# An order table, v through SyncE's queue, ungated weights and a re-cut w_out in a fused attention and MLP kernel

## Chip, cores and metric

The kernel runs on one core of a Trainium2 chip. The metric is device time of one execution in microseconds (us), the median of three runs.

## What is computed

For batch b and head h a state of 48 x 48 runs over 768 steps: the output at a step is r times (state + (u k) v), then the state becomes w times state + k v. The result, reordered to 3072 tokens of 384 values, goes through two matrix products.

```python
y[:, :, t] = einsum('bhd,bhde->bhe', rt, state + einsum('bhd,bhe->bhde', u[None] * kt, vt))
state = w[None, :, :, None] * state + einsum('bhd,bhe->bhde', kt, vt)
...
h = x @ w_in                 # 384 -> 2048
g = maximum(h, 0) ** 2
out = g @ w_out              # 2048 -> 384
```

The inputs and the output are f32. r, k and v have the shape (4, 8, 768, 48).

## The kernel before, in words

The 768 steps are cut into 6 chunks of 128, and chunk times batch gives 24 **units** (unit i is chunk i // 4, batch i % 4). All state and product work of a unit is done by matmuls over its 128 steps. For each unit the steps are, with the names that the texts below use (the order table's words are the same):

- `rt`, `kt`, `vt`: loads of r, k and v, 192 KB each (lines 430 and 462). r and k go through SyncE's (SP's) hardware queue. Units 0 to 5 load r and k in two halves of 96 KB with long runs, units from 6 on with runs of 192 bytes. v goes through GpSimd's (POOL's) software queue in all units. Before each v load from unit 2 on, POOL copies one element of the k of the unit before (line 465, `gate`), so that v does not start before that load has landed.
- `scale` (DVE, line 453): r and k times powers of w, to bf16.
- Transposes of the scaled r and k. In units 0 to 5 TensorE (PE) does it: `turn` (line 481), eviction `rkT` by ScalarE (ACT), a turn back `kb` with its eviction `kbT`. In units from 6 on a DMA transpose on SP's queue does it (line 473, `rkD` in the table of the change).
- `at` (line 515): eight matmuls over 64 rows. `mask` (DVE, two per unit), `rk` (DVE).
- `sums` (line 535, `s` in the table): four narrow matmuls for the diagonal, four for the new state. `dv`, `sadd`, `sdec` on DVE, `stb` on ACT follow. `vb` (ACT, line 469) casts v to bf16; it is needed by `sums` and `y`.
- `y` (line 569): the output, evicted by `yb` (DVE). It is turned by PE with `xturn` and `xT` in units 0 to 5, by a DMA transpose on SP (`xD`, line 599) in the others.
- `m1` (line 613): four groups of 12 matmuls per unit, weights from `w_in`. Group s uses quarter s of w_in, called I.s. `relu` (ACT) and the squares `sq` (`sqA` on ACT, `sqD` on DVE) follow each group.
- `m2` (line 642): four groups of four matmuls per unit of 384 columns. Group q uses quarter q of w_out, called O.q. `osb` (ACT) evicts, `out` stores through SP's queue. The last unit is done in two halves (line 658).

The eight weight quarters are cast to bf16 by DMAs of POOL's queue (line 441). A `gate` copy ahead of each one waits for some load of r or k (FRONT, line 277).

Every instruction is issued in an order that is worked out when the program is traced: class `Plan` (line 17) holds the steps with costs, ranks and needs, walks a planned clock and emits the steps. `TURNS` (line 197) has ranks that were changed by hand. Engines run their own instruction queues in order: an instruction that waits holds up all that stand behind it on that engine. While PE has nothing to do at the start, the planner puts in `fill` matmuls (line 379, one 128x128 each), 98 in all. `place` says which of eight PSUM banks a step writes.

In the order before, POOL's queue has: vt.0, the mask, vt.1, zeros, the columns of u (`uwb`), vt.2, I.0, vt.3, I.1, `wend`, I.3, I.2, vt.4, O.0 to O.3 and vt.5 on; the weights that each call loads follow the planner's ranks.

Of the kernel before, what the change touches and what calls it, by code (L numbers as in the profile page):

```python
# [16 lines left out]
class Plan:  # L17

    def __init__(self, lags, cold, spare, turns):
        self.turns = turns
        self.lags = lags
        self.cold = cold  # L30
        self.spare = spare
        self.steps = []
        self.at = {}
        self.users = {}
        self.place = {}

    def add(self, key, engine, cost, emit, needs=(), rank=0.0, new=(), uses=(), move=None):
        kind, which = (key[0], key[1] if len(key) == 2 else key[1:]) if isinstance(key, tuple) else ("", key)
        rank = self.turns.get(kind, {}).get(which, rank)
        s = dict(key=key, engine=engine, cost=cost, emit=emit, rank=rank, new=new, move=move)  # L40
        s["needs"] = [n for n in needs if n is not None]
        self.at[key] = s
        self.steps.append(s)
        for x in tuple(new) + tuple(uses):
            self.users.setdefault(x, []).append(s)

    def run(self, room, banks, count):
        todo = {}
        for s in self.steps:
            todo.setdefault(s["engine"], []).append(s)  # L50
        for mine in todo.values():
            mine.sort(key=lambda s: s["rank"])
        rings = {name: [] for name in room}
        free = {e: 0.0 for e in todo}
        queues = {e: [] for e in todo}
        held = {n: None for n in range(count)}
        since = {n: 0.0 for n in range(count)}
        begin, until, tight, loose = self.spare
        free["SP"] = 0.74
        held[0] = "fill"  # L60
        order = []
        t = 0.0
        left = len(self.steps)
        tiny = 1e-9

        moved, chained, left_pe, to_pe, near = self.lags

        def ready(s, e):
            if s["move"]:
                return s["end"] + moved + s["move"][4]  # L70
            if s["engine"] == "PE":
                return s["end"] + (chained if e == "PE" else left_pe)
            return s["end"] + (to_pe if e == "PE" else near)

        marks = []

        def mark(s):
            for e in ("PE", ""):
                heappush(marks, ready(s, e))

        def done(s, e):
            return "end" in s and ready(s, e) <= t + tiny

        def fits(s):
            e = s["engine"]
            names = [x[0] for x in s["new"]]
            for name in set(names):
                if name in banks:
                    continue
                ring, m = rings[name], room[name]  # L90
                for n in range(len(ring) - m, len(ring) - m + names.count(name)):
                    if n >= 0 and not all(done(x, e) for x in self.users[ring[n]]):
                        return False
            wanted = [name for name in names if name in banks]
            if wanted:
                for n, x in held.items():
                    if x not in (None, "fill") and all(done(u, e) for u in self.users[x]):
                        held[n], since[n] = None, max(u["end"] for u in self.users[x])
                if sum(x is None for x in held.values()) < len(wanted):
                    return False  # L100
                for name in set(wanted):
                    mine = sum(x is not None and x[0] == name for x in held.values())
                    if mine + wanted.count(name) > banks[name]:
                        return False
            return True

        while left:
            if held[0] == "fill" and t > until:
                held[0] = None
            for e, mine in todo.items():  # L110
                if free[e] > t + tiny:
                    continue
                if e == "PE" and t < begin - tiny:
                    free[e] = begin
                    continue
                for s in mine:
                    if s["move"] and sum(x[1] / x[0]["move"][0] * x[0]["move"][3] for x in queues[e]) > 1.5:
                        continue
                    if all(done(self.at[k], e) for k in s["needs"]) and fits(s):
                        mine.remove(s)  # L120
                        left -= 1
                        for x in s["new"]:
                            if x[0] in banks:
                                n = 4 + x[1] if x[0] == "log" else min((n for n in held if held[n] is None), key=lambda n: since[n])
                                held[n] = x
                                self.place[x] = n
                            else:
                                rings[x[0]].append(x)
                        s["start"] = t
                        free[e] = t + s["cost"] * (self.cold[1] if e == "PE" and t < self.cold[0] else 1.0)  # L130
                        if s["move"]:
                            queues[e].append([s, s["move"][0], free[e] + s["move"][2]])
                        else:
                            s["end"] = free[e]
                            mark(s)
                        order.append(s)
                        break
                else:
                    if e == "PE" and t < until:
                        free[e] = t + (tight * self.cold[1] if t < self.cold[0] else loose)  # L140
                        order.append(dict(key="fill", emit=self.fill, start=t, end=free[e], engine="PE"))
            heads = [q[0] for q in queues.values() if q]
            moving = [x for x in heads if x[2] <= t + tiny]
            whole = sum(x[0]["move"][1] for x in moving)
            later = [f for f in free.values() if f > t + tiny]
            while marks and marks[0] <= t + tiny:
                heappop(marks)
            later += marks[:1]
            later += [x[2] for x in heads if x[2] > t + tiny]
            later += [t + x[1] * whole / x[0]["move"][1] for x in moving]  # L150
            if not later:
                if left:
                    raise ValueError("nothing can go on: " + str([s["key"] for m in todo.values() for s in m[:3]]))
                break
            step = min(later) - t
            t += step
            for x in moving:
                x[1] -= step * x[0]["move"][1] / whole
                if x[1] <= 1e-7:
                    queues[x[0]["engine"]].pop(0)  # L160
                    x[0]["end"] = t
                    mark(x[0])
        return order
# [3 lines left out]
def kernel(  # L167
# [26 lines left out]
    LATE = (0.2, 0.2, 0.4)  # L194
    MOST = 3
    SQUARES = 'AAAMAAAM'
    TURNS = {
        "": {
            "zeros": 38.551
        },  # L200
        "O": {
            0: 76.019, 1: 91.228, 2: 107.535, 3: 7
        },
        "rt": {
            0: -83.003, 1: -66.162, 12: 22.377, 13: 28.231, 14: 28.49, 15: 33.657, 3: -36.29, 5: 1.476, 8: 3.237
        },
        "kt": {
            0: -80.584, 1: -55.486, 10: 19.508, 11: 20.529, 2: -47.443, 6: 2.358
        },
        "at": {  # L210
            0: -3.958, 11: 34.671, 4: -16.745, 7: 10.944
        },
        "mask": {
            (1, 0): -39.238, (10, 0): 33.02, (2, 1): 25.375, (5, 1): 1.515
        },
        "sadd": {
            1: 9.124, 4: 45.244
        },
        "rk": {
            2: 13.012, 7: 14.32, 8: 68.867, 9: -12.042  # L220
        },
        "sums": {
            11: 49.353, 2: -24.778, 8: 5.082
        },
        "dv": {
            2: -26.848, 7: 34.164, 9: -12.993
        },
        "stb": {
            2: -9.741, 4: 57.421
        },  # L230
        "scale": {
            (10, 0): 23.594, (11, 0): -15.371, (3, 0): -29.763, (4, 0): 33.082, (7, 1): 6.517, (8, 1): 4.379
        },
# [656 lines left out]
```

## Time and profile before

| what | value |
|---|---|
| median of 3 runs (lowest, highest) | 176.56 us (176.39, 176.58) |
| profiled execution, first to last instruction (span) | 174.3 us |
| what lies around the span, by the median | 2.26 us |
| PE busy | 166.7 us, 96% |
| ACT busy, DVE busy, POOL busy | 132.1, 121.1, 40.0 us |
| DMA packets, data | 76474, 28.93 MB |
| share of 16 DMA engines: SP's queue, POOL's queue | 69.8%, 23.9% |

The profiled execution has no time of its own on the page beside its span, so the distance to the median is the difference of the two. PE is TensorE's matmuls, PEld its weight loads, which lie beside the matmuls. The names with a q behind (POOLq, SPq) are the engines' queues that issue DMAs. The chain of waits is followed back from the last instruction to what released it. "To landing" is the time from the issue of a DMA to its completion. The DMA share adds up the times of packets, so it can be above 1 where two queues are served in turn.

### The profile page before, as it was taken

To read this page: it belongs to the slowest core of one execution; us is meant where nothing else is said; L and a number is where in the kernel's file an instruction comes from. 1 tells how busy PE (TensorE), PEld (TensorE's weight loads), DVE (VectorE), ACT (ScalarE), POOL (GpSimd) and SP (SyncE) were. 2 spreads that over 40 slices of the span, in tenths; PEclk is the share of its full clock that TensorE was granted. 3 is DMA by queue.
4 is the path that set the end of the run, shared out by engine and by line. 5 is a ranking of instruction groups with operands and counts; after the bars stand their busy time and mean duration, and the time that the engine had idled before them with its cause. 6 is when DMAs were issued, how large, how long until landed. Compare 5 with 4: busy or idle time off the path is not lost.

```text
span 174.3 us, 5795 instructions
## 1 busy us (share of the span) xinstructions
PE 166.7 (96%) x2390; PEld 134.7 (77%) x2390; DVE 121.1 (70%) x252; ACT 132.1 (76%) x268; POOL 40.0 (23%) x84
## 2 busy tenths in 40 slices
PE   7978899999999999999999999999999999999991
PEld 6766799887687787886896787869787698877871
DVE  7869976615999899977986799794989635531010
ACT  3946999999458797886968876939994869948640
POOL 7866890300140220302032202203202000000000
PEclk9999999999999999999999999999999999999999
DMA  4889999999999999999999999999999971130121
GB/s 97 228 179 246 232 218 193 185 221 118 170 201 164 178 154 209 200 214 170 231 142 183 156 237 214 218 177 141 186 200 175 271 180 26 26 111 6 47 81 56
DMA packets 76474, 28.93 MB, mean 166 GB/s; under 512 B 65440, under 2 KB 75296, under 8 KB 76448
## 3 DMA queue, kind: packets, MB, share of 16 engines
q1 hardware_dynamic: 70848, 20.56, 69.8%
q0 software_dynamic: 5312, 7.87, 23.9%
q8 instruction: 18, 0.29, 0.8%
q10 hardware_dynamic: 288, 0.15, 0.4%
q14 instruction: 8, 0.07, 0.1%
HBM read 20.50 MB, written 4.72 MB: 145 GB/s over the span
## 4 chain that ended last, share of the span: by engine, by line
PE 81%; DMA 11%; SPq 4%; issue 1%; DVE 0%; POOL 0%; POOLq 0%
PE bank L623 35%; PE bank L647 33%; DMA w_in_q<-in_moe_w_in_dram 5%; SPq L436 4%; DMA rkT<-rkw 4%; PE bank L521 4%; DMA rt<-in_r_dram 2%; PE bank L576 2%; PE bank L582 2%; PE bank L546 2%; PE bank L663 2%; PE bank L541 1%; PE bank L487 0%; PE bank L607 0%; POOL gate L442 0%
## 5 line engine op out<-in xcount | busy, mean ns | idle before, releaser
L623 PE MATMUL bank<-xT,w_in_q 128*128 128x128 bf16 x1152 | 70.7, 219 | 0.1
L623 PEld LDWEIGHTS <-w_in_q 128*128 128x128 bf16 x1152 | 66.5, 98 | 3.1 <-DMA w_in_q<-in_moe_w_in_dram 0.3
L647 PE MATMUL bank<-w_out_q,g 128*128 128x384 bf16 x368 | 66.9, 326 | 0.0
L631 ACT ACTIVATE gr<-bank 128x512 f32<-128x512 f32 x96 | 54.3, 599 | 13.6 <-PE bank L623 13.3
L647 PEld LDWEIGHTS <-g 128*128 128x128 bf16 x368 | 33.3, 98 | 19.8
L638 ACT ACTIVATE g<-gr 128x512 bf16<-128x512 f32 x72 | 43.7, 637 | 0.4
L533 DVE TENSOR_TENSOR am<-bank,smask 128x512 bf16<-128x512 f32 x48 | 31.3, 682 | 3.3 <-PE bank L521 3.1
L640 DVE TENSOR_TENSOR g<-gr 128x512 bf16<-128x512 f32 x24 | 16.5, 686 | 21.5 <-ACT gr L631 21.5
L465 POOL COPY gate<-kt 128x1 f32<-128x1 f32 x22 | 5.8, 266 | 80.9 <-DMA kt<-in_k_dram 80.9
L654 ACT COPY osb<-bank 128x384 f32<-128x384 f32 x23 | 11.0, 483 | 15.8 <-PE bank L647 15.8
L467 POOL DMA_DIRECT2D vt<-in_v_dram x24 | 21.4, 893 | 5.9 <-issue 1.6
L555 DVE TENSOR_TENSOR dv<-vb,bank 128x384 f32<-128x384 bf16 x24 | 13.2, 548 | 5.3 <-PE bank L546 3.4
L513 DVE TENSOR_TENSOR rk<-rkT 128x512 bf16<-128x512 bf16 x24 | 10.0, 417 | 7.7 <-DMA rkT<-rkw 4.3
L591 DVE TENSOR_TENSOR yb<-bank,dv 128x384 bf16<-128x384 f32 x24 | 13.2, 550 | 2.8 <-PE bank L582 2.4
L471 ACT CAST vb<-vt 128x384 bf16<-128x384 f32 x24 | 12.4, 518 | 0.0
L458 DVE TENSOR_TENSOR rkw<-rt,wpos 128x384 bf16<-128x384 f32 x18 | 9.8, 550 | 1.4 <-DMA rt<-in_r_dram 1.4
L458 DVE TENSOR_TENSOR rkw<-kt,wneg 128x384 bf16<-128x384 f32 x18 | 9.9, 549 | 0.9 <-DMA kt<-in_k_dram 0.9
L567 ACT CAST stb<-st 128x384 bf16<-128x384 f32 x20 | 10.4, 519 | 0.0
L380 PE MATMUL bank<-warm 128*128 128x128 bf16 x98 | 9.3, 248 | 1.1 <-DVE warm L322 1.1
L521 PE MATMUL bank<-rkT 64*128 64x128 bf16 x192 | 9.5, 219 | 0.2
L494 ACT COPY rkT<-bank 128x512 bf16<-128x512 bf16 x12 | 6.8, 588 | 3.0 <-PE bank L487 3.0
L563 DVE TENSOR_TENSOR st<-st,wend 128x384 f32<-128x384 f32 x16 | 8.8, 549 | 0.0
(74 smaller groups left out, 129.1 us busy)
## 6 DMA issues: line engine op xcount, KB each, us to landing
vt<-in_v_dram POOLq DMA_DIRECT2D x24, 192.0 KB, 4.6
out_dram<-osb SPq DMA_DIRECT2D x23, 192.0 KB, 4.0
rt<-in_r_dram SPq DMA_DIRECT2D x18, 192.0 KB, 4.5
kt<-in_k_dram SPq DMA_DIRECT2D x18, 192.0 KB, 4.3
w_in_q<-in_moe_w_in_dram POOLq DMA_DIRECT2D x4, 384.0 KB, 7.9
w_out_q<-in_moe_w_out_dram POOLq DMA_DIRECT2D x4, 384.0 KB, 12.7
kt<-in_k_dram SPq DMA_DIRECT2D x12, 96.0 KB, 4.3
rt<-in_r_dram SPq DMA_DIRECT2D x11, 96.0 KB, 4.2
```

Of the source, the lines that this page charges most:

```text
L458: nc.vector.tensor_tensor(t["rkw"][:, x, :, :, :D], pair(src), pair(wneg if x else wpos), ALU.mult)
L467: nc.gpsimd.dma_start(out=tiles[i]["vt"], in_=v[b, :, c * C : (c + 1) * C, :].rearrange("h s d -> s h d"))
L471: nc.scalar.copy(tiles[i]["vb"], tiles[i]["vt"])
L521: nc.tensor.matmul(out=t["at"][o][:, p, :], lhsT=t["rkT"][sl, 1, p, :], rhs=t["rkT"][sl, 0, p, :], start=True, stop=True,)
L533: nc.vector.tensor_tensor(am, t["at"][o], smask.unsqueeze(1).to_broadcast([C, HP, C]), ALU.mult)
L555: nc.vector.tensor_tensor(t["dv"], t["vb"], t["d"].unsqueeze(2).to_broadcast([C, H, D]), ALU.mult)
L591: nc.vector.tensor_tensor(t["yb"], t["y"], t["dv"].rearrange("p h d -> p (h d)"), ALU.add)
L623: nc.tensor.matmul(out=t["h", s][:, a], lhsT=turned, rhs=chunks[c]["xT"][:, n, b : b + m, :], start=(n == 0), stop=(n == NK - 1),)
L631: nc.scalar.activation(t["gr", s], t["h", s], AF.Relu)
L638: nc.scalar.activation(g, x, AF.Square)
L640: nc.vector.tensor_tensor(g, x, x, ALU.mult)
L647: nc.tensor.matmul(out=t["o"], lhsT=chunks[units[i][0]]["g"][:, f, units[i][1], :], rhs=w_out_q[f // 4][:, f % 4, :], start=(f == 0), stop ...
```

## The change

The planner is gone. Its place is taken by a string `ORDER` in which each word is one step, as `m1.0.2@4`: name, unit, part and, behind the @, the PSUM bank. A loop goes through the words and emits them. The engines' orders are those of the table, and differ from before throughout.

- v of units 6 to 23 is loaded through SP's queue (`vtS`); v of units 0 to 5 stays on POOL's, with no gate copy.
- The weight loads have no gate copies. POOL's order is I.0, the identities, vt.0, the mask, vt.1, zeros, vt.2, uwb, wend, vt.3, I.2, I.1, O.0, I.3, O.1, O.2, O.3, vt.4, vt.5, and then nothing.
- w_out's quarter is laid out so that each partition holds four adjacent rows (one run of 6 KB in place of four of 1.5 KB). To match, `m1` takes every fourth column of its w_in quarter as weights, at a step of 4 elements (8 bytes).
- The first half of the load of k of unit 1 is issued by ACT (`ktA`).
- The identities are made behind I.0. `sums` stays one step; the code has an unused way to do its two parts apart.
- There are 105 fills in place of 98.

```diff
+ORDER = """
+kt.0.0 kt.0.1 rt.0.0 rt.1.0 I.0 rt.1.1 ids fill.25 log@4567 ktA.1.0 lnat.0 kt.1.1 vt.0 lnat.1 w.0 fill.1 cols@1
+rt.2.0 w.1 upper copied rt.2.1 end scale.0.0 wk rt.3.0 vt.1 scale.0.1 wr rt.3.1 fill.16 turn.0.0@2 zeros turn.0.1@3
+kt.2.0 rkT.0.0 vt.2 rkT.0.1 uwb scale.1.0 kt.2.1 fill.16 kb.0@1 rk.0 at.0@45 kbT.0 turn.1.0@6 wend mask.0.0 kt.3.0
+rkT.1.0 mask.0.1 vb.0 vt.3 vb.1 scale.1.1 kt.3.1 fill.20 s.0@7 I.2 y.0@2 sadd.0 fill.4 turn.1.1@3 kt.4.0 vb.2 dv.0
+I.1 stb.0 scale.2.0 rt.4.0 rkT.1.1 O.0 yb.0 rt.4.1 fill.17 turn.2.0@1 scale.3.0 I.3 fill.1 kb.1@4 rkT.2.0 rt.5.0
+xturn.0@6 rk.1 at.1@57 kbT.1 scale.2.1 O.1 turn.3.0@3 kt.4.1 xT.0 mask.1.1 vb.3 fill.5 s.1@2 kt.5.0 O.2 turn.2.1@1
+mask.1.0 rkT.3.0 m1.0.0@4 kt.5.1 O.3 rkT.2.1 dv.1 y.1@0 kt.6 scale.3.1 relu.0.0 vt.4 kb.2@6 yb.1 at.2@73 sqA.0.0
+turn.3.1@5 sadd.1 rt.5.1 kbT.2 xturn.1@1 mask.2.1 rkT.3.1 m1.0.2@4 vt.5 mask.2.0 xT.1 kb.3@0 stb.1 rk.3 at.3@26
+relu.0.2 m1.1.0@3 rk.2 mask.3.0 kbT.3 sqA.0.2 s.2@5 scale.4.0 vtS.6 y.2@1 s.3@7 relu.1.0 dv.2 m1.1.2@4 sadd.2
+sqA.1.0 turn.4.0@0 yb.2 m1.0.1@2 relu.1.2 mask.3.1 stb.2 m1.1.1@3 sqA.1.2 sadd.3 xturn.2@5 relu.0.1 dv.3 y.3@1
+m2.0.0@4 scale.4.1 xT.2 stb.3 yb.3 m2.1.0@6 sqA.0.1 turn.4.1@7 rkT.4.0 m1.2.1@2 relu.1.1 xturn.3@5 rkT.4.1 m1.2.2@1
+sqA.1.1 rk.4 m1.2.0@0 relu.2.2 kb.4@3 relu.2.1 m1.0.3@7 kbT.4 sqA.2.1 m1.1.3@1 relu.0.3 m2.0.1 relu.1.3 sqD.0.3
+at.4@23 relu.2.0 m2.1.1 sqD.1.3 xT.3 mask.4.0 sqA.2.0 m1.2.3@7 sqA.2.2 mask.4.1 m2.1.2 relu.2.3 m1.3.0@1 vtS.7
+sqD.2.3 m1.3.2@0 relu.3.0 m1.3.3@5 sqA.3.0 rt.6 m1.3.1@2 relu.3.2 vb.4 m2.1.3 rt.7 sqA.3.2 s.4@3 scale.5.0 vb.5
...
+m2.23.1@1
+osb.23.0 out.23.0 osb.23.1 out.23.1
+"""
...
-    def weights(gated, q, which):
-        nc.gpsimd.tensor_copy(gate, tiles[gated[1]][gated[0]][:, H - 1, :1])
+    def weights(which, q):
...
-            src = moe_w_out.rearrange("(q a ki) d -> q ki a d", q=NQ, a=NF // NQ)
+            src = moe_w_out.rearrange("(q ki a) d -> q ki a d", q=NQ, a=NF // NQ)
...
+    def load_v(i, queue=None):
+        c, b = units[i]
+        if i >= VGATE and queue is None:
             nc.gpsimd.tensor_copy(gate, tiles[i - 1]["kt"][:, H - 1, :1])
         tiles[i]["vt"] = loads.tile([C, H, D], F32, name="vt")
+        (queue or nc.gpsimd).dma_start(out=tiles[i]["vt"], in_=v[b, :, c * C : (c + 1) * C, :].rearrange("h s d -> s h d"))
...
-                turned = w_in_q[f // 4][:, n, f % 4 * 128 : f % 4 * 128 + 128]
+                turned = w_in_q[f // 4][:, n, f % 4 :: 4]
...
+        vt=load_v, vtS=lambda i: load_v(i, nc.sync), vb=cast_v,
...
+    for word in ORDER.split():
+        what, _, where = word.partition("@")
+        name, *a = what.split(".")
+        if name == "fill":
+            for _ in range(int(a[0])):
+                fill()
+            continue
+        a = [int(x) for x in a]
+        if where:
+            place.update(zip(names(name, *a), (int(x) for x in where)))
+        steps[name](*a)
```

More of the change, by code (lines that the diff above doesn't have):

```diff
@@ L1 @@
 from contextlib import ExitStack
-from heapq import heappop, heappush
 import concourse.bass as bass
@@ L14 @@
 PSUM = bass.MemoryType.PSUM
[L17 to L163, printed above, removed]
@@ new lines @@
+vb.7 sdec.4 m2.3.0@6 osb.0 kt.8 scale.6.0 xturn.4@2 stb.4 m2.2.0@3 scale.6.1 xT.4 out.0 sqA.3.1 m2.2.1 scale.7.0
+rkT.5.1 rkD.6 m1.4.0@1 relu.3.3 rk.5 scale.7.1 m1.4.3@7 relu.4.0 sqD.3.3 kt.9 at.5@42 sqA.4.0 m1.4.2@0 mask.5.1
+relu.4.3 vtS.8 kb.5@5 mask.5.0 relu.4.2 m1.4.1@1 sqD.4.3 kbT.5 m2.2.2 vtS.9 sqA.4.2 m2.2.3 relu.4.1 scale.8.0 rt.9
+y.5@2 sqA.4.1 s.5@7 scale.8.1 osb.2 m2.3.1 rkD.7 sadd.5 m2.4.0@4 dv.5 sdec.5 m2.4.1 out.2 yb.5 rkD.8 stb.5 at.6@05
+rk.6 m2.4.2 mask.6.0 kt.10 s.6@1 mask.6.1 m2.3.2 vb.8 dv.6 xturn.5@3 y.6@7 sadd.6 rt.10 xT.5 m2.4.3 vb.9 yb.6
@@ new lines @@
+sadd.11 m1.9.1@1 osb.7 sqD.8.3 m1.9.2@3 vb.14 out.7 mask.11.0 relu.9.1 vtS.15 m1.9.3@5 dv.11 relu.9.2 kt.14
+scale.13.0 y.11@0 sqA.9.1 m1.8.2@6 scale.13.1 sqA.9.2 sdec.11 m1.9.0@2 relu.9.3 kt.15 yb.11 stb.11 m2.8.0@7
+scale.14.0 xD.11 relu.8.2 sqD.9.3 m2.8.1 relu.9.0 scale.15.0 m1.10.1@1 sqA.8.2 kt.16 sqA.9.0 rkD.13 m1.10.2@4
+relu.10.1 rk.12 at.12@35 relu.10.2 m2.8.2 mask.12.0 kt.17 sqA.10.1 m2.9.0@0 mask.12.1 sqA.10.2 m2.9.1 vb.15 kt.18
+y.12@6 scale.14.1 s.12@2 m2.8.3 rt.16 sadd.12 m1.10.3@1 dv.12 osb.8 sdec.12 rkD.14 m1.11.3@4 relu.10.3 scale.15.1
@@ L683, in store @@
         nc.sync.dma_start(out=out[b * S + c * C : b * S + (c + 1) * C, :], in_=tiles[i]["osb"])
-    PE, ACT, DVE, POOL, SP = "PE", "ACT", "DVE", "POOL", "SP"
-    L1, L2 = 7, 18
-    def late(n, i):
-        return min(MOST, LATE[n] * max(0, i - NPE))
-    def do(fn, *a):
-        return lambda: fn(*a)
-    add = copy = plan.add
-    plan.fill = fill
-    add("w0", ACT, 3.2, None, rank=-1e3)
-    add("log", PE, 0.28, spread_log, rank=-1e3, needs=["w0"], new=[("log", n) for n in range(4)])
-    for x in range(2):
-        add(("lnat", x), DVE, 0.47, do(log_at, x), rank=-1e3 + x, needs=["w0", ("lnat", 0) if x else None])
-        add(("w", x), ACT, 0.42, do(power_four, x), rank=-1e3 + x, needs=[("lnat", x)])
@@ L704 @@
-    add("wk", ACT, 0.48, do(power, wneg, down), rank=-999, needs=["log", ("w", 1)], uses=[("log", n) for n in range(4)])
-    add("wr", ACT, 0.48, do(power, wpos, up), rank=-998, needs=["wk"], uses=[("log", n) for n in range(4)])
-    add("wu", POOL, 3.85, None, rank=-1e3)
-    add("upper", POOL, 0.9, upper, rank=-998, needs=["wu"])
-    add("zeros", POOL, 0.5, zeros, rank=-996, needs=["upper"])
-    add("cols", PE, 0.15, spread_columns, rank=-50, needs=["upper"], new=[("h", "cols")])
-    add("copied", DVE, 0.1, copy_columns, rank=-50, needs=["cols"], uses=[("h", "cols")])
@@ L854, with names @@
-    room = dict(
-        rt=7, kt=7, vt=7, rkw=NPAD, g=2, rkT=6, vb=NVB, rk=4, am=8, dv=4, yb=4, xT=3, gr=6, osb=6,
-    )
-    for s in plan.run(room, dict(at=4, s=2, y=2, h=5, o=2, log=4), 8):
-        if s["emit"] is not None:
-            s["emit"]()
+    def names(name, *a):
+        if name == "log":
+            return [("log", n) for n in range(4)]
+        if name == "at":
+            return [("at", a[0], o) for o in range(2)]
+        if name == "m2":
+            return [("o", *a)] if a[0] == NU - 1 else [("o", a[0])]
+        if name in ("s", "y", "d"):
+            return [(name, *a)]
+        return [dict(cols=("h", "cols"), turn=("h", a[0], "rk", *a[1:]), kb=("h", *a[:1], "kb"), xturn=("h", *a, "x"), m1=("h", *a))[name]] if a else [("h", "cols")]
@@ new lines @@
+    steps = dict(
+        log=spread_log, lnat=log_at, w=power_four, wk=lambda: power(wneg, down), wr=lambda: power(wpos, up),
+        ids=identities, upper=upper, zeros=zeros, cols=spread_columns, copied=copy_columns, uwb=u_columns,
+        end=end_columns, wend=end_blocks, I=lambda q: weights("I", q), O=lambda q: weights("O", q),
+        rt=lambda *a: load("rt", *a), kt=lambda *a: load("kt", *a), ktA=lambda *a: load("kt", *a, nc.scalar), rtA=lambda *a: load("rt", *a, nc.scalar),
+        vt=load_v, vtS=lambda i: load_v(i, nc.sync), vb=cast_v, vbP=lambda i: cast_v(i, nc.gpsimd.tensor_copy), scale=scale, turn=turn, rkT=lambda i, x=None: evict_rk(i, x), rkD=turn_dma, kb=turn_back, kbT=evict_back, d=lambda i: diag_sums(i, bank("d", i)[:, :H]),
+        rk=rk, at=at, mask=mask, s=sums, dv=diag_v, sadd=state_add, sdec=state_decay, stb=state_cast,
+        y=y_mm, yb=evict_y, xturn=x_turn, xT=evict_x, xD=x_dma,
+        m1=lambda i, s: mm1(i, size(i), s), relu=lambda i, s: relu(i, size(i), s),
+        sqA=lambda i, s: square(i, size(i), s, True), sqD=lambda i, s: square(i, size(i), s, False),
+        m2=lambda i, q: mm2(i, q) if i < NU - 1 else mm2_half(i, q),
+        osb=lambda i, n=None: evict_o(i) if n is None else evict_half(i, n),
+        out=lambda i, n=None: store(i) if n is None else store_half(i, n),
+    )
```

357 lines of the change are left out of this document (90 added, 267 removed).

## The prediction

> **What bounds the kernel now.** I cut the span in three by the view of windows, at the moment when the chain of waits enters the matmuls for good and at the one when it leaves them.
>
> ```profile
> 0.00:21.96 21.96, 18.13 (x281) 15.15 (x282) 17.96 (x52) 15.56 (x33) 16.42 (x42) 1.00 0.89 197
> 21.96:170.76 148.80, 148.52 (x2109) 119.51 (x2109) 102.88 (x201) 116.50 (x236) 23.58 (x43) 1.00 0.98 164
> 170.76:174.30 3.54, 0.00 (x0) 0.00 (x0) 0.29 (x1) 0.00 (x0) 0.00 (x0) 1.00 0.18 58
> ```
>
> The columns are the length, busy time of PE, PEld, DVE, ACT and POOL, the clock, the DMA share and GB/s. From 21.96 us on PE is busy 148.52 of 148.80 us at the full clock. That stretch holds matmuls that the change neither removes nor adds; only those done earlier leave it. So the gain, if any, lies in the first 22 us. The chain says what they wait for, and what a group of matmuls costs when PE never stops:
>
> ```profile
> 8.82 4.27 DMA rt<-in_r_dram
> ...
> 13.73 8.19 DMA w_in_q<-in_moe_w_in_dram
> ...
> 25.02 0.22 PE bank L487 x4
> ...
> 26.58 0.33 PE bank L521 x8
> ...
> 27.18 0.22 PE bank L502 x4
> ...
> 29.42 0.20 PE bank L576 x8
> ...
> 30.46 0.08 PE bank L541 x4
> 30.54 0.19 PE bank L546 x4
> 30.73 0.67 PE bank L623 x12
> ...
> 33.39 0.17 PE bank L607 x3
> ```
>
> The head hangs on r of unit 2 (landed at 13.1) and then on the second quarter of w_in, I.1: its gate waits for that load, it is issued at 13.73 and lands at 21.92. How much real work PE had done by then is in its groups up to 21.95 us:
>
> ```profile
> L380 PE MATMUL bank<-warm 128*128 128x128 bf16 x98 | 9.3, 248 | 1.1 <-DVE warm L322 1.1
> L487 PE MATMUL bank<-identb,rkw 128*128 128x128 bf16 x36 | 3.4, 221 | 2.0 <-DVE rkw L460 1.9
> L623 PE MATMUL bank<-xT,w_in_q 128*128 128x128 bf16 x24 | 1.7, 219 | 0.0
> L521 PE MATMUL bank<-rkT 64*128 64x128 bf16 x32 | 1.6, 219 | 0.0
> L502 PE MATMUL bank<-identb,rkT 128*128 128x128 bf16 x16 | 1.6, 219 | 0.0
> L546 PE MATMUL bank<-vb,rkw 128*128 128x96 bf16 x16 | 1.3, 205 | 0.0
> L576 PE MATMUL bank<-vb,am 128*128 128x48 bf16 x24 | 1.1, 183 | 0.0
> L607 PE MATMUL bank<-identb,yb 128*128 128x128 bf16 x9 | 1.0, 222 | 0.4 <-DVE yb L591 0.3
> ```
>
> At the chain's paces: m1 2 x 0.67, turn 9 x 0.22, at 4 x 0.33, kb 4 x 0.22, sums 4 x 0.27 (0.08 + 0.19), y 3 x 0.20, xturn 3 x 0.17, together 7.7 us in 22. The rest is fills and waits.
>
> **A ledger for the order table.** In the table PE has ahead of its first m1 group (m1.0.0) seven turns, two kb, two at, two sums, one y and one xturn: 1.54 + 0.44 + 0.66 + 0.54 + 0.20 + 0.17 = 3.55 us. Behind it remain 148.8 + 7.7 - 3.55 = 152.95 us, then the tail of 3.54, which keeps its form (two halves of m2.23), and the 2.26 us between span and median (176.56 - 174.3; the profiled execution has no other time of its own, so I put the median beside it). Hence
>
> time = t + 158.75,
>
> where t is the start of m1.0.0 plus all later waits beyond the 0.28 us that before has too. Before stands at t = 17.8; that is the point of no change. It remains to work out t.
>
> *Earliest t.* These are the fills, and the first POOL and ACT steps that matter:
>
> ```profile
> 1.06 2.63 PE L380 MATMUL bank<-warm 128*128 128x128 bf16 x23 [1.06 <-DVE warm L322]
> 3.69 0.76 PE L392 MATMUL four<-lnw,ones 32*128 32x96 f32 x8
> ...
> 7.92 1.00 PE L380 MATMUL bank<-warm 128*128 128x128 bf16 x15
> ```
>
> ```profile
> 2.90 0.09 POOL masks.py:197 MEMSET ident<- 4x4 f32 x1
> ...
> 3.70 0.93 POOL L467 DMA_DIRECT2D vt<-in_v_dram  x1
> ...
> 5.48 0.92 POOL L467 DMA_DIRECT2D vt<-in_v_dram  x1
> ...
> 7.34 0.71 POOL L419 CAST uwb<-cols 64x4 bf16<-64x4 f32 x2
> ...
> 14.47 0.95 POOL L428 COPY wend<-wend_c 64x192 f32<-64x192 f32 x2
> ```
>
> Taking off the last fill's own 0.25 us, 23 early fills cost 0.108 each, 15 later ones (1.00 - 0.25) / 14 = 0.054. The table's 105: 25 early ones 2.7, 16 in between 1.3 (taken at 0.08), 64 late ones 3.5. With the start at 1.06, the spread of the logs and columns (0.8) and 3.55 of work, m1.0.0 could start at 12.9 us. The seven fills more cost 7 x 0.054 = 0.4, in this sum already.
>
> *v behind I.0.* Ungated, I.0 goes into POOL's queue at 2.9, ahead of vt.0. Its rows before, and the first cast of v:
>
> ```profile
> L445 POOL DMA_DIRECT2D w_in_q<-in_moe_w_in_dram x1: 744/744/744, 10.4 to 10.4; - x1
> ...
> DMA to landing us min/median/max: 5.8/5.8/5.8
> ```
>
> ```profile
> 8.00 0.51 ACT L471 CAST vb<-vt 128x384 bf16<-128x384 f32 x1
> ```
>
> So I.0 lands near 2.9 + 5.8 = 8.7 and vt.0 some 0.9 us behind (POOL's queue is served in order; the rate follows below): vb.0 starts at 9.6 in place of 8.0. ACT's order is vb.0, vb.1, vb.2, stb.0, rkT.1.1, so that rkT.1.1 and the casts of unit 1's keys stand behind vt.2, near 11.4. Three ACT steps later, at 0.45 each (22 steps in 9.96 us, row below), rkT.1.1 is done at 12.8 and kb.1 starts at 13.1, where fills and work alone would have it at 11.2. With 1.7 us of work and fills behind kb.1, m1.0.0 starts at 14.8.
>
> ```profile
> 30.00:40.00 10.00, 10.00 (x133) 8.19 (x131) 4.80 (x9) 9.96 (x22) 1.55 (x2) 1.00 1.24 200
> ```
>
> *The other weights.* This is the last part of POOL's queue before:
>
> ```profile
> L448 POOL DMA_DIRECT2D w_out_q<-in_moe_w_out_dram x4: 740/742/760, 20.6 to 23.2; - x4
> ...
> DMA to landing us min/median/max: 9.9/12.7/15.5
> ```
>
> From I.1 (21.92) to the last O (23.2 + 15.5 = 38.7) six quarters and vt.4 landed in 16.8 us; a v load counted as a third of a quarter, one takes 2.65. POOL reaches I.2 at 11.6: from 2.90 on, 0.74 for I.0, 0.80 for the identities, 1.78 for vt.0 and the mask (5.48 - 3.70), 2.57 for vt.1, zeros and uwb (8.05 - 5.48), 0.95 for wend, 2 x 0.93 for vt.2 and vt.3. It lands by 17.4 if it takes I.0's 5.8, and at 15.0 if it only follows vt.2 by a v load and a quarter (11.4 + 0.9 + 2.65). Its slot is 1.8 us of work behind m1.0.0, at 16.6. ACT asks for the same: ten steps behind rkT.1.1 is rkT.3.1, done at 17.3, which kb.3 needs, 2.5 us behind m1.0.0 at best. Short waits for DVE (mask.1.0 to y.1, rk.2 to s.2) I put at 0.4. That gives t = 16.0: 14.8, plus 0.8 for I.2 at the late end and ACT together, plus 0.4. Then I.1, O.0, I.3, O.1, O.2, O.3 land 2.65 apart from 17.4 on, at 20.1 to 33.3, and vt.4 and vt.5 at 34.2 and 35.1; by the table's work, their first users stand at t + 5.4, 7.1, 11.0, 12.3, 14.6, 18.0, 18.0 and 18.9, so 21.4 to 34.9. All are met, the last ones with nothing to spare.
>
> *v on SP's queue.* 18 more issues in order. What SP moves now takes:
>
> ```profile
> kt<-in_k_dram SPq DMA_DIRECT2D x18, 192.0 KB, 4.3
> ...
> rkT<-rkw SPq DMA_TRANSPOSE x18, 4.5
> xT<-yb SPq DMA_TRANSPOSE x18, 4.1
> ```
>
> I add up PE's work in the table between issue and first use: rkD to at 6.4 us or more, xD to m1 5.3, vtS to vb 5.1. The medians fit with 0.8 to 1.9 us to spare. Behind a late rkD on SP stand the next loads and xD, behind a late v ACT's whole list. The DMA share of 0.98 says that nothing is free here. I put 0.25 on it; its ends are 0 and 4 (four late transposes by a spare each). The POOL gates cost nothing before (80.9 us of waits, but on an idle engine), so their end gains nothing by itself. ktA takes ACT's 0.6 us wait for lnat; without that cover it would cost 0.6.
>
> *w_out and strided weights.* I take the longer runs at nothing: the w_out quarters land 2.7 apart before, no row shows 6 KB runs, and the ends are a gain of 1 per quarter and a loss of 0.2. For the strided weight load, no row has a step; the nearest are these:
>
> ```profile
> L623 PEld LDWEIGHTS <-w_in_q 128*128 128x128 bf16 x1152 | 66.5, 98 | 3.1 <-DMA w_in_q<-in_moe_w_in_dram 0.3
> ...
> L392 PEld LDWEIGHTS four<-lnw,ones 32*128 32x128 f32 x8 | 0.5, 305 | 0.3 <-ACT lnw L351 0.3
> ```
>
> A load of 98 ns goes every 56 ns (0.67 / 12), so it is overlapped. Lower end 0, upper end one load of 98 ns per matmul: 1152 x 42 ns = 48 us. I take 0, by the bf16 row. The Trainium skill, "TensorE: Matmul & The Clock Gate", section on weight-path perf modes, says that the fast weight load takes a column step up to 1,024 elements; by that the sum stays. No run here shows it. The same page's plain rule of columns / 1.2 ns would make it 107 ns a matmul, by my estimate 59 us more.
>
> **Sum:** t = 16.0 + 0.25, time = 175.0 us.
>
> **The rivals.**
>
> - *Best case (0.18).* vt.0 to vt.2 land soon enough (POOL's queue has bigger packets and little beside it at 3 to 9 us), and t is 13 to 14.5: 171.7 to 173.3. For it speaks vt.0's early landing before, against it ACT, 9.96 of 10 us busy at 30 to 40.
> - *POOL's queue is the bound (0.22), the other side.* vt.5 lands at 17.4 + 6.67 x, x the time of a quarter. At 2.65 it just meets vb.5; above 2.9 it lands behind 36.7, where before would have been, and all of ACT's list waits behind vb.4 and vb.5. At 3.1 it is 38.1, so t = 19.2 and 178.0 us. For: SP's queue has vtS.6 and vtS.7 beside it now. Against: longer runs.
> - *SP is late in the middle (0.08):* four waits of 1 us, 178.8.
> - *Strided loads do not overlap (0.04):* up to 223.
> - *Ledger right, but head waits eat it all (0.08):* within 0.2%, 176.2 to 176.9, about what a measurement of this kernel can tell from no change.
>
> The forecast holds 0.40, its own range is 173.4 to 176.1. The range of 171.7 to 178.8 leaves out the strided case, half of SP's and the worst of the queue's, 0.12 in all. Faster: 0.40 + 0.18 = 0.58; same 0.08; slower 0.22 + 0.08 + 0.04 = 0.34.
>
> **What would show it.** m1.0.0 near 15 (17.6 before); vb.0 near 9.6; I.2 landing by 17.4; a 12-group of m1 still 0.67 us; vt.5 landed by 35; PE without a gap from some 20 us on, and no waits for rkT or vt beyond 1 us. A pace of m1 above 0.67, or an ACT wait for vt.4 or vt.5, would make it wrong.

## The result, and the profile after

The changed kernel takes 184.67 us (median of four runs, 184.45 to 188.55) beside 176.47 us for the kernel before: 1.048 times the time, 95% interval 1.044 to 1.052. The forecast was 175.0 us, the range ended at 178.8. The profiled execution took 184.5 us with a span of 182.6. Ratios here and below leave disturbed runs out (188.55 is one), so they need not be the quotient of two medians.

First the chain by engine of the page after:

```profile
PE 63%; DMA 23%; POOL 3%; ACT 3%; issue 2%; DVE 2%; SPq 2%; POOLq 0%; ACTq 0%
PE bank L473 26%; PE bank L497 25%; DMA vt<-in_v_dram 9%; DMA xT<-yb 7%; DMA rkT<-rkw 7%; PE bank L354 3%; PE bank L426 2%; PE bank L513 1%; PE bank L383 1%; PE bank L432 1%; DVE am L362 1%; POOL vt L300 1%; SPq L309 1%; PE bank L320 1%; PE bank L395 1%
```

The chain no longer runs into matmuls and stays there. 23% of it is DMA, in three kinds: v, turned x and turned r and k. In order of time (start, length, what), the DMA pieces over 2.9 us are:

```profile
7.68 7.05 DMA vt<-in_v_dram
...
77.37 4.80 DMA xT<-yb
...
86.65 4.54 DMA rkT<-rkw
...
98.05 4.88 DMA vt<-in_v_dram
...
103.94 3.61 DMA xT<-yb
...
116.88 5.17 DMA rkT<-rkw
...
126.84 3.60 DMA vt<-in_v_dram
...
133.43 3.17 DMA rkT<-rkw
138.74 4.51 DMA xT<-yb
```

One is in the head, eight are between 77 and 143 us. The windows say how much PE lost there. These are rows of after, cut where the last turned x lands (155.3 us: its transpose is issued at 152.9 and takes 2.4); columns as in the prediction.

```profile
22.00:155.30 133.30, 126.67 (x1861) 101.17 (x1859) 103.24 (x201) 102.65 (x204) 0.00 (x0) 1.00 0.92 174
155.30:182.60 27.30, 23.85 (x282) 19.14 (x280) 3.06 (x5) 17.73 (x36) 0.00 (x0) 1.00 0.12 45
```

And of before, cut at its last x (issued at 153.9, landed at 156.3):

```profile
22.00:156.30 134.30, 134.06 (x1953) 108.25 (x1954) 101.45 (x198) 107.33 (x219) 23.54 (x43) 1.00 1.07 176
156.30:174.30 18.00, 14.42 (x159) 11.22 (x156) 1.68 (x3) 9.13 (x18) 0.00 (x0) 1.00 0.16 56
```

Two things are to be seen. PE is idle for 133.30 - 126.67 = 6.63 us of the middle, where before has 0.24. And the last x lands at nearly the same moment in both kernels, 155.3 and 156.3 us, with the same DMA rate (174 and 176 GB/s); but behind it stand 23.85 us of PE's work in the table's order and 14.42 in the planner's. 9.4 us more work behind a landing 1.0 us earlier is the 8.3 us by which the span grew.

That sum says where the time went, not yet why. In before PE is busy all the way up to its last x, so there the planner's order sets the 156.3, not a landing. The loads say it more directly: the last one lands at 137.0 us in before (a v, issued at 131.0) and at 137.9 in after (a k, issued at 134.7). The rows from there to the end, of after and of before:

```profile
137.93:182.60 44.67, 40.59 (x558) 33.45 (x556) 15.96 (x30) 30.16 (x58) 0.00 (x0) 1.00 0.26 70
137.00:174.30 37.30, 33.66 (x436) 26.76 (x430) 12.20 (x22) 24.02 (x48) 0.00 (x0) 1.00 0.29 82
```

The loads end 0.9 us later, and 7.4 us more pass behind them.

### The profile page after: what moved, and what is told of

Read it like the earlier page. It is cut to its first block, busy times and chain, and to the rows that moved or that the text cites. A ratio compares the mean times of both kernels' runs of the same rounds, so it can differ in the third digit from the quotient of the medians.

```text
span 182.6 us, 5704 instructions
## 1 busy us (share of the span) xinstructions
PE 168.6 (92%) x2397; PEld 136.3 (75%) x2397; DVE 121.9 (67%) x252; ACT 134.7 (74%) x268; POOL 16.2 (9%) x36
## 4 chain that ended last, share of the span: by engine, by line
PE 63%; DMA 23%; POOL 3%; ACT 3%; issue 2%; DVE 2%; SPq 2%; POOLq 0%; ACTq 0%
PE bank L473 26%; PE bank L497 25%; DMA vt<-in_v_dram 9%; DMA xT<-yb 7%; DMA rkT<-rkw 7%; PE bank L354 3%; PE bank L426 2%; PE bank L513 1%; PE bank L383 1%; PE bank L432 1%; DVE am L362 1%; POOL vt L300 1%; SPq L309 1%; PE bank L320 1%; PE bank L395 1%
## 5 line engine op out<-in xcount | busy, mean ns | idle before, releaser
L473 PE MATMUL bank<-xT,w_in_q 128*128 128x128 bf16 x1152 | 73.1, 219 | 3.3 <-DMA xT<-yb 3.3
L473 PEld LDWEIGHTS <-w_in_q 128*128 128x128 bf16 x1152 | 67.7, 114 | 7.5 <-DMA xT<-yb 4.8
L497 PE MATMUL bank<-w_out_q,g 128*128 128x384 bf16 x368 | 68.8, 326 | 0.1
L481 ACT ACTIVATE gr<-bank 128x512 f32<-128x512 f32 x96 | 54.9, 606 | 10.3 <-PE bank L473 9.3
L488 ACT ACTIVATE g<-gr 128x512 bf16<-128x512 f32 x72 | 44.7, 645 | 0.8
L405 DVE TENSOR_TENSOR dv<-vb,bank 128x384 f32<-128x384 bf16 x24 | 13.1, 544 | 1.1 <-PE bank L383 1.1
L354 PEld LDWEIGHTS <-rkT 64*128 64x128 bf16 x192 | 5.4, 94 | 7.9 <-DMA rkT<-rkw 5.1
L210 PE MATMUL bank<-warm 128*128 128x128 bf16 x105 | 9.8, 260 | 1.1 <-DVE warm L154 1.1
L409 DVE TENSOR_TENSOR st<-bank,st 128x384 f32<-128x384 f32 x16 | 8.8, 549 | 2.6 <-PE bank L383 2.6
L210 PEld LDWEIGHTS <-warm 128*128 128x128 bf16 x105 | 8.3, 120 | 1.2 <-DVE warm L154 1.0
```

What stands on the lines that cost most here:

```text
L210: nc.tensor.matmul(out=banks[0][:, :128], lhsT=warm, rhs=warm, start=True, stop=True)
L354: nc.tensor.matmul(out=t["at"][o][:, p, :], lhsT=t["rkT"][sl, 1, p, :], rhs=t["rkT"][sl, 0, p, :], start=True, stop=True,)
L405: nc.vector.tensor_tensor(t["dv"], t["vb"], t["d"].unsqueeze(2).to_broadcast([C, H, D]), ALU.mult)
L473: nc.tensor.matmul(out=t["h", s][:, a], lhsT=turned, rhs=chunks[c]["xT"][:, n, b : b + m, :], start=(n == 0), stop=(n == NK - 1),)
L481: nc.scalar.activation(t["gr", s], t["h", s], AF.Relu)
L488: nc.scalar.activation(g, x, AF.Square)
```

## The experiments

| kernel | median us | ratio to before, 95% interval | last x lands | PE work behind it | PE idle from 22 us to it |
|---|---|---|---|---|---|
| before | 175.5 to 176.5 | 1 | 156.3 | 14.4 | 0.2 |
| after | 184.67 | 1.048 (1.044 to 1.052) | 155.3 | 23.9 | 6.6 |
| after, another chip | 185.26 | 1.054 (1.045 to 1.063) | 158.0 | 23.9 | 8.9 |
| v on POOL, no gates | 183.76 | 1.038 (1.030 to 1.046) | 154.2 | 23.8 | 5.3 |
| v on POOL, gates | 185.20 | 1.042 (1.033 to 1.051) | 157.3 | 23.8 | 9.6 |
| v on ACT's queue | 181.33 | 1.030 (1.024 to 1.037) | 152.0 | 23.9 | 3.5 |
| half of v | 177.81 | 1.012 (1.005 to 1.018) | 147.0 | 23.9 | 0.4 |
| half of k | 179.78 | 1.019 (1.010 to 1.028) | 150.0 | 23.9 | 2.9 |
| v in two issues | 187.93 | 1.057 (1.048 to 1.067) | 156.0 | 23.9 | 8.2 |
| v in long runs | 189.07 | 1.076 (1.068 to 1.084) | 160.0 | 23.9 | 9.0 |
| v later in the order | 182.99 | 1.041 (1.038 to 1.043) | 156.2 | 23.8 | 6.1 |
| I.0 behind vt.2 | 183.68 | 1.043 (1.034 to 1.051) | 154.2 | 23.9 | 6.1 |
| planner's order, v on SP | 177.40 | 1.013 (1.006 to 1.019) | 156.8 | 14.5 | 1.6 |
| planner's order, all other parts | 178.14 | 1.010 (1.007 to 1.013) | 157.2 | 14.5 | 0.8 |
| before, no weight gates | 176.34 | 1.003 (0.999 to 1.007) | 156.0 | 14.5 | 0.0 |
| the same, w_out cut anew | 176.82 | 0.999 (0.995 to 1.003) | 155.9 | 14.5 | 0.2 |

Each row has its own profiled execution; those of the gated v on POOL, of the later v and of after on the other chip took 186.2, 185.6 and 187.2 us, above their medians, so their last three columns are read for the place of the loss, not for tenths. The head differs between executions of one order too: m1.0.0 starts at 17.2 to 19.1 us in kernels with the same words up to it.

**Is it v in SP's queue?** First theory: yes (A), by the ring's pace or its order; rival: the table's distances are too short (C). The v loads went back to POOL at the table's places:

```diff
-        vt=load_v, vtS=lambda i: load_v(i, nc.sync), vb=cast_v,
+        vt=load_v, vtS=lambda i: load_v(i, nc.gpsimd), vb=cast_v,
```

> The kernel after, with v of units 6 to 23 issued by POOL at the same places of the table, without gates; all else as after (184.6 us). Theory A (v in SP's queue makes the transposes late, either by SP's order of issue or by the one ring's pace): the waits for rkT, xT and vt between 77 and 144 us, some 7 us together, go; 177.5 us, between 176.8 and 178.5, the head as after. Theory C (the table asks too early for the transposes, whatever queue v is in): 183 to 185 us, waits for rkT and xT as in after, at 82, 104, 122 and 138 us.

Neither came out clean. PE's waits for the transposes shrank to 2 us, near 88 us. But PE stood still for 3.5 us up to 42.4, because the second half of rt.5 landed at 41.75, and from 43 to 47 us its granted clock was 0.50 to 0.67, where after has 1.00: by my estimate from these windows another 1.7 us. The chain of this kernel has it as one piece, and SP's timeline (start, length) shows it and what stood behind it:

```profile
18.10 23.65 DMA rt<-in_r_dram
```

```profile
17.44 0.61 SPq L271 DMA_DIRECT2D kt<-in_k_dram  x1
18.10 3.72 SPq L273 DMA_DIRECT2D rt<-in_r_dram  x1
21.86 6.19 SPq L271 DMA_DIRECT2D rt<-in_r_dram  x2
28.15 12.95 SPq L271 DMA_DIRECT2D kt<-in_k_dram  x1
```

An issue of the kind that takes 0.61 us in the first row held SP for 12.95 us while POOL's queue carried the weights and, with no gate, one load of v after the other. So this kernel exchanged one loss for another. The second try has gates:

```diff
-            nc.gpsimd.tensor_copy(gate, tiles[i - 1]["kt"][:, H - 1, :1])
+            nc.gpsimd.tensor_copy(gate, tiles[max(j for j in range(NU) if "kt" in tiles[j])]["kt"][:, H - 1, :1])
...
-        vt=load_v, vtS=lambda i: load_v(i, nc.sync), vb=cast_v,
+        vt=load_v, vtS=load_v, vb=cast_v,
```

> The kernel after, with v of units 6 to 23 on POOL's queue at the same places of the table, each behind a gate copy that waits for the last k load that the table has issued so far. With v on POOL and no gates the waits behind 100 us had gone, but 5 us were lost near 42 us, where one issue of SP took 12.95 us. Theory A (two queues side by side carry it, and those 5 us came from v loads that started at once): 176.5 to 178.5 us, no wait near 42 us. Theory C (the table's distances are too short with either queue): 181 us or more, with waits for rkT and xT behind 77 us.

185.2 us: theory A falls; v on POOL's queue is no cure in either of these two forms. Now it is v that comes late for ACT (us in total, times, longest), and PE waits for what ACT does behind it (6.2 us for xT and g of ACT, 2.8 for the DMA transposes):

```profile
ACT vb L304 <- DMA vt<-in_v_dram: 17.1, 13, 4.0
```

The queue of v alone, in the kernel before (v's gate copies of these units go with it):

```diff
-        if i > 1:
+        if 1 < i < 6:
             nc.gpsimd.tensor_copy(gate, tiles[i - 1]["kt"][:, H - 1, :1])
...
-        nc.gpsimd.dma_start(out=tiles[i]["vt"], ...)
+        (nc.gpsimd if i < 6 else nc.sync).dma_start(out=tiles[i]["vt"], ...)
```

> The kernel before (176.5 us) with one part of the change alone: v of units 6 to 23 through SP's queue, issued where the planner's order put them for POOL. Theory A: the transposes come late here too; PE gets waits for rkT and xT behind 60 us, 179 to 184 us. Theory C: the planner's order has enough distance, 176.3 to 177.3 us.

1.9 us more than before, under theory A's 179 and 0.1 above C's range: v on SP's queue costs something in the planner's order too, but only about a quarter of what after lost.

**Is it the number of issues, the packets, the ring or the data?** Four variations of the v loads of units 6 on, in the kernel after.

```diff
-        (queue or nc.gpsimd).dma_start(out=tiles[i]["vt"], in_=v[b, :, ...
+        n = 4 if queue else H
+        (queue or nc.gpsimd).dma_start(out=tiles[i]["vt"][:, :n], in_=v[b, :n, ...
...
+                tiles[i]["vt"][:, :4].rearrange("p h d -> p (h d)").unsqueeze(1).to_broadcast([C, 2, 4 * D]),
```

> The kernel after; for units 6 to 23 only heads 0 to 3 of v are loaded, one issue each of half the packets, and the cast writes these four heads to both halves of vb (the other four heads' v is left out). Theory A1 (the number of issues in SP's order is what counts, some 0.55 us each): 183 to 185 us. Theory A2 (the data counts: packets of 192 bytes of v in the one ring, about 1 us of all DMA engines per load, 18 us in all, half of it gone): half or more of the 7 us of waits goes, 179.5 to 181.5 us.

177.8 us, lower than A2 had it: PE runs almost without a wait (0.4 us) once 1.77 of the 24 MB of SP's queue are gone.

```diff
+        for h in (0, 4) if queue else (0,):
+            n = 4 if queue else H
+            (queue or nc.gpsimd).dma_start(
+                out=tiles[i]["vt"][:, h : h + n], in_=v[b, h : h + n, ...
```

> The kernel after; each v load of units 6 to 23 is issued in two halves of four heads, same packets and data, 18 more issues on SP. Theory A1 (number of issues): 18 more at about 0.55 us on a queue that is back to back, 188 to 194 us. Theory A2 (data): 184 to 185.5 us.

The ratio, 1.057, is that of after (1.048, and 1.054 on another chip) within the intervals of the table. 18 more issues cost nothing that can be told, and half of v, with as many issues as after, had been far below A1's 183: A1 falls.

```diff
+        for o in range(2):
+            queue.dma_start(out=tiles[i]["vt"][:, o * 4 : o * 4 + 4].rearrange("p h d -> p (h d)"), in_=halves(src)[o])
```

> The kernel after, with v of units 6 to 23 read on SP's queue in two issues with runs of 768 bytes, as r and k of the first units are: same data, a quarter of the packets; the rows come in another order, so that v is not the right one for the step. Theory A2 (packets of 192 bytes cost the ring its time): 177 to 180 us. Theory A4 (bytes, or the place in the ring's order, count): as with two issues of short runs, 184 to 188 us.

A2's wording falls here: with a quarter of v's packets the kernel is slower, 1.076, although its DMA share from 100 to 120 us is 0.67 where after has 0.97. So the time for which 192-byte packets keep the engines busy is not what holds the loads up. Why long runs are slower than short ones stays open.

```diff
+        vtS=lambda i: load_v(i, nc.scalar)
```

> The kernel after, with v of units 6 to 23 issued by ACT on a hardware queue of its own, same places of the table, same packets of 192 bytes. Theory A3 (what counts is that v stands in SP's ring ahead of the transposes): waits behind 77 us go; 177 to 180 us, with some loss from 18 issues of some 0.6 us on ACT. Theory A2 (the 16 DMA engines' pace on packets of 192 bytes, whatever the ring): the waits stay, 183 to 187 us.

Between the two. A ring of its own takes half of the idle time away (3.5 us left). The Trainium skill, "DMA: Bandwidth & Descriptors", section "Issuing engines are not separate DMA queues", says that transfers of all issuing engines end on the same 16 DMA engines and interleave; the loss that stays with v outside SP's ring, here and on POOL, agrees with it, but the half that went does not follow from it.

Last, is it v at all, or any data?

```diff
-            nc.sync.dma_start(out=t[name], in_=src.rearrange("h s d -> s h d"))
+            n = 4 if name == "kt" else H
+            nc.sync.dma_start(out=t[name][:, :n], in_=src[:n].rearrange("h s d -> s h d"))
...
```

> The kernel after; for units 6 to 23 only heads 0 to 3 of k are loaded and scaled into both halves (the other heads' k is left out); v is whole, on SP's queue, the table as it is. Theory Q (the table asks SP's queue for more data by a given moment than it brings, whichever data it is): as with half of v, 176.5 to 179 us, last turned x near 147 us. Theory V (v itself counts, by its place or its cast on ACT): 182 to 185 us, with waits for vt and for the transposes.

> The kernel after itself, unchanged, beside the runs of before on this chip: 183.5 to 185.5 us by its first measurement. It is the base for the kernel with half of k.

5.5 us below after on the same chip, v untouched. That is 0.8 us above theory Q's range and 2.2 below V's. With half of v at 1.012 and half of k at 1.019, whose intervals overlap, it is mostly the amount of data, whichever it is. The windows of the kernels with half of v and half of k, cut at their last x:

```profile
22.00:147.00 125.00, 124.56 (x1842) 100.47 (x1840) 101.58 (x199) 101.83 (x202) 0.00 (x0) 1.00 0.91 172
147.00:174.40 27.40, 23.91 (x284) 19.20 (x281) 3.06 (x5) 17.82 (x36) 0.00 (x0) 0.98 0.12 45
```

```profile
22.00:150.00 128.00, 125.06 (x1846) 100.42 (x1843) 101.80 (x200) 101.75 (x203) 0.00 (x0) 1.00 0.93 168
150.00:177.50 27.50, 23.91 (x284) 19.21 (x281) 3.06 (x5) 17.81 (x36) 0.00 (x0) 1.00 0.12 44
```

The rate hardly moves, 172 and 168 GB/s; what moves is when the data are there. With half of v the last load lands at 130.0 us, with half of k at 133.1, in after at 137.9. Seven profiles have v on SP's queue and the table's order behind the head: after twice, half of v, half of k, two issues, long runs, and I.0 behind vt.2 (below). In all of them 43.8 to 44.7 us pass from the landing of the last load to the end. The table is a schedule in which the last load lands by 130 and the last x by 147.

**Is it the place of v in SP's order?** For units 8 on, `vtS` was put behind its unit's `rkD` and `vb` ahead of `at`:

```diff
-... vtS.16 m1.11.1@6 ... vtS.17 scale.16.0 ... rkD.16 ... vb.16 ... at.16@50
+... m1.11.1@6 ... scale.16.0 ... rkD.16 vtS.16 ... vb.16 at.16@50
```

> The kernel after with 16 words of the table moved twice: for units 8 to 23, vtS stands right behind rkD of its unit (28 to 148 words later) and vb right ahead of at or s of its unit; all other words keep their order, same data, same queue. Theory P (v of far units stands in SP's order ahead of transposes that are needed at once): the rkD come earlier; at least half of the 7 us of waits goes, 178 to 181 us. Theory Q (the data that SP's queue has to carry by a given moment is too much, whatever its order): the transposes gain only what the v loads lose; 183 to 186 us, with at and s waiting for vb.

Theory P falls: 182.99 is above its 181, and at the lower end of Q's range. The ratio of 1.041 lies under after's 1.048, so the move won about 1 us of the 8. In after PE waited 3.0 us for rkT and 3.3 for xT, and not for vb, behind 22 us; in this kernel (us in total, times, longest):

```profile
PE bank L353 <- DMA rkT<-rkw: 2.1, 3, 1.1
PE bank L472 <- DMA xT<-yb: 2.1, 2, 1.0
PE bank L382 <- ACT vb L303: 1.4, 1, 1.4
```

The transposes gained 2.1 us, and 1.4 came back as a wait for vb.

**Is it the order table?** All parts of the change but the table, in the kernel before with its planner and TURNS; the gates go for the weights and for v:

```diff
-        nc.gpsimd.tensor_copy(gate, ...)
+        (nc.gpsimd if i < 6 else nc.sync).dma_start(out=tiles[i]["vt"], ...)
+            src = moe_w_out.rearrange("(q ki a) d -> q ki a d", ...)
+                turned = w_in_q[f // 4][:, n, f % 4 :: 4]
```

> All parts of the change but the order table (and ktA, which is in the table): the kernel before with its planner's order, v of units 6 to 23 on SP's queue, no gates, w_out by adjacent rows with strided w_in columns. Theory T (the order table is the cause: the last turned x lands at 155 to 157 us in the kernels with either order, but 23.9 us of PE's work stand behind it in the table's order and 14.5 us in the planner's): 176.5 to 179 us, last x at 155 to 158 us. Theory V (v in SP's queue costs the 7 us, in any order, once the weights are ungated and w_out is cut anew): 181 to 185 us.

Its windows:

```profile
22.00:157.20 135.20, 134.43 (x1954) 108.75 (x1955) 102.19 (x198) 107.89 (x219) 0.00 (x0) 1.00 0.96 174
157.20:175.00 17.80, 14.54 (x162) 11.36 (x159) 1.68 (x3) 9.15 (x18) 0.00 (x0) 1.00 0.16 57
```

This is theory T. Same loads on the same queues (but for ktA), same 174 GB/s, last load at 138.8 and last x even 1.9 us later than in after, and yet 1.010 in place of 1.048: 14.5 us of work are left behind the last x in place of 23.9, and PE was idle for 0.8 us up to it in place of 6.6. Without the table nearly four fifths of the loss are gone; v on SP's queue with the planner's order (1.013 alone, 1.010 here) costs about 1%. The shares need not add up, since half of v under the table takes most of the loss away too: the table and the amount of data make it together.

**The other parts.** The gates, and with them the cut of w_out:

> The kernel before without the eight gate copies ahead of the weight loads; all else as before. Theory T: a few tenths either way, 175 to 177 us, with I.0 landing by 14 us in place of 16.2 and I.1 by 20 in place of 21.9, m1.0.0 up to 2 us earlier. Rival G (weights that start at once take the engines from r, k and v of the first units): scale and vb of units 1 to 3 come later, 177 to 179 us.

> The kernel before without the eight gate copies and with the new cut of w_out (6 KB runs) and strided w_in columns. If the strided weight loads are overlapped, it lies within 0.7 us of the kernel without gates alone, 174.5 to 177 us, with an m1 group of 12 at 0.67 us and O.0 to O.3 some 2.1 us apart in place of 2.7. If they cost, as the mean of 114 ns in place of 98 may hint, a group of 12 takes over 0.67 us, and the time is 178 us or more.

```diff
-        nc.gpsimd.tensor_copy(gate, tiles[gated[1]][gated[0]][:, H - 1, :1])
```

(The second has the lines of w_out and w_in of the kernel above as well.) Neither differs from before by what can be measured. Without gates I.0 landed at 15.7 (not by 14: it stands behind vt.2, which landed at 13.0), I.1 at 19.6, and m1.0.0 still began at 18.0. The groups of m1 without and with strided weights:

```profile
L622 PE MATMUL bank<-xT,w_in_q 128*128 128x128 bf16 x1152 | 70.7, 219 | 0.0
L622 PEld LDWEIGHTS <-w_in_q 128*128 128x128 bf16 x1152 | 66.5, 98 | 2.8
```

```profile
L622 PE MATMUL bank<-xT,w_in_q 128*128 128x128 bf16 x1152 | 70.7, 219 | 0.1
L622 PEld LDWEIGHTS <-w_in_q 128*128 128x128 bf16 x1152 | 67.5, 113 | 2.8 <-issue 0.3
```

A strided load takes 113 ns in place of 98 and is covered: the matmuls' 70.7 us are the same. The longer runs brought O.0 to O.3 in 2.1 us each (28.2 to 34.5) in place of 2.9 (28.3 to 36.9).

**The head.** I.0 moved from ahead of vt.0 to behind vt.2:

```diff
-... rt.1.0 I.0 rt.1.1 ... vt.2 rkT.0.1 ...
+... rt.1.0 rt.1.1 ... vt.2 I.0 rkT.0.1 ...
```

> The kernel after, with the first quarter of w_in (I.0) issued behind vt.2 in place of ahead of vt.0. Theory H1 (the head is late because vt.0 to vt.2 stand behind I.0): vb.0 starts near 8 us in place of 12.1, and m1.0.0 comes at 15.5 to 17 in place of 18.06; the whole 182.5 to 184.6 us, since the queue behind is the limit from 77 us on. Theory H2 (I.0 is then what m1.0.0 waits for, or r and k are what is late): m1.0.0 at 17.5 to 19, 184 to 186 us.

m1.0.0 came at 15.70 and the whole at 183.68, as H1 has them. But the next v is then behind I.0, as ACT's row says, and PE's granted clock fell, as the window does:

```profile
16.07 0.52 ACT L304 CAST vb<-vt 128x384 bf16<-128x384 f32 x1 [1.96 <-DMA vt<-in_v_dram]
```

```profile
19.00:20.00 1.00, 1.00 (x12) 1.00 (x11) 1.00 (x3) 0.96 (x4) 0.88 (x1) 0.50 1.25 244
```

By 21.5 us all but 0.3 us of the lead of 2.4 was gone. ACT's list stood behind vt.3, and PE was idle for 0.6 us; the granted clock, 0.50 from 18 to 21 us (1.00 there in after), took about 1.7 us by my estimate. Why it fell is not shown. Two more executions, at the full clock, took 182.94 and 183.98 us, so the lead does not reach the end there either. No version here beats the kernel before.

## Why the prediction was wrong, point by point

**The ledger** holds as a sum, to 1.2 us. With m1.0.0's start (18.06) and PE's idle time behind it (0.2 up to 22 us, 6.6 to the last x, less the 0.28 of before) it gives 183.3 of 184.5 us; PE's work behind m1.0.0 is 154.3 us where the ledger has 152.7. Both terms of t were off: the head's 16.0 by 2.2, and SP's 0.25 by 6.1.

**The term for v on SP's queue, "I put 0.25 on it",** is the step that failed, and with it the price of "SP is late in the middle": that rival was of the right kind, but it was given four waits of 1 us and a chance of 0.08, and it was nine waits for transposes, 6.3 of the 6.6 us. I compared the distances in the table (6.4, 5.3 and 5.1 us of PE's work) with times from issue to landing. The landings were even shorter than I took:

```profile
vt<-in_v_dram SPq DMA_DIRECT2D x18, 192.0 KB, 3.9
...
rkT<-rkw SPq DMA_TRANSPOSE x18, 3.6
xT<-yb SPq DMA_TRANSPOSE x18, 3.0
```

What was wrong is the start. I counted from the word's place, as if SP reached it when PE did. (I worked out what follows from the starts of the instructions in the traces.) The issue of rkD, measured against the start of the next matmul step in the table, comes 0.8 us early for unit 6, 3.1 late for unit 12, 4.6 for unit 16 and 6.0 for unit 19; with half of v it is 0.8 early, then 0.9, 1.6 and 3.8 late. A distance of 6.4 less 4 to 6 does not hold a landing of 3.6. So the waits of after:

```profile
ACT vb L304 <- DMA vt<-in_v_dram: 9.4, 9, 2.5
...
DVE rkw L291 <- DMA rt<-in_r_dram: 6.0, 7, 1.5
PEld L354 <- DMA rkT<-rkw: 5.1, 7, 1.7
PEld L473 <- DMA xT<-yb: 4.8, 5, 1.5
```

v's loads, r's loads and both transposes are late, in turn.

**"So the gain, if any, lies in the first 22 us"** was the deeper mistake. It took the 148.8 us behind as work that any order can pack as tightly. PE hardly stopped behind 22 us in before, but its loads lasted until 137.0 us all the same; the planner's order had work to do meanwhile, and the table keeps 7 us more of it for afterwards. Before's own trace had the number: its last load at 137.0 and the table's 44 us behind a last load come to 181, against a span of 182.6; the 44 is read from the runs with the table. (The sum by the last x, 156.3 + 27.3 = 183.6, comes as near, but with luck: 156.3 was set by the planner's order.) Both sums were made afterwards. I quoted the share of 0.98 and wrote "nothing is free here", then sized the term by slack.

**The head** failed by size. I.0 landed at 10.55 (8.7 forecast), vt.0 to vt.2 at 12.06, 13.19 and 14.74 (11.4 for the last). I had taken 0.9 us for a v load, worked out from POOL's queue at 22 to 39 us; here they come 1.4 apart. The mechanism is as told: the chain goes vt.2, vb.2, stb.0, rkT.1.1, kb.1.

```profile
7.68 7.05 DMA vt<-in_v_dram
14.76 0.51 ACT vb L304
15.27 0.41 ACT stb L417
15.69 0.49 ACT rkT L327
...
16.23 0.40 PE bank L335 x4
```

kb.1 (L335) starts at 16.23 where I had 13.1, and m1.0.0 at 18.06 where I had 14.8.

**Right** were: the strided loads at no cost and a pace of 0.67, the gates at nothing, and that ACT does not wait for vt.4 and vt.5. That vt.5 landed at 35.4 us, forecast 35.1, is luck: I.2 landed at 19.0 (17.4 forecast), and the six quarters behind it then came 2.33 apart on the mean in place of 2.65. The longer runs, which I had taken at nothing, made up for it with 0.8 us a quarter of w_out. By the Trainium skill's rule of the column step, cited in the prediction ("TensorE: Matmul & The Clock Gate", section on weight-path perf modes), the load stays fast; the traces agree for the pace (the matmuls' rows above), but the mean of a load rose from 98 to 114 ns in after:

```profile
L473 PEld LDWEIGHTS <-w_in_q 128*128 128x128 bf16 x1152 | 67.7, 114 | 7.5 <-DMA xT<-yb 4.8
```

**Open** stays what limits the stream at 168 to 180 GB/s (180 with v on ACT's ring): neither the number of issues nor the packets of v, and SP's ring only in part. The planner's order, whose last x is due near 156, carries v on SP's queue at 1.010 to 1.013; a table made for such a landing was not tried, and neither was this table with all of before's queues and gates.

## What to carry to other kernels

A busy engine can hide a stream that is just as full. Before trusting a new order, take from the old trace when the last load lands and add the time that the new order needs from there to the end; if that sum is longer than the forecast, the order is tuned to a stream that isn't there. And slack on an in-order queue counts from when the queue gets to the issue, not from the word's place in a table.

## What the runs showed of the hardware

- One DMA issue on SP took 12.95 us (0.61 for one of the same kind), and an r load ahead of it landed 23.65 us after its own issue, while POOL's queue moved weights and v without gates.
- v in runs of 768 bytes (two issues) was slower than in runs of 192 (1.076 to 1.057), at a lower DMA share.
- A bf16 weight load at a step of 4 elements takes 113 ns in place of 98, and with the planner's order none of it shows in the matmuls (70.7 us for 1152 either way).
- The granted clock of TensorE fell to 0.50 for some us in single profiles, as from 44 to 46 us with ungated v on POOL, behind a stop of PE of 3.5 us, and from 18 to 21 us with I.0 behind vt.2.
